# Attention, low-rank token mixing, a two-layer product and a gated projection on one core: weights of the first group prepared in attention, sums of u kept in DRAM, value weights and gates moved in the job list

## The chip, the cores and the metric

One core of one Trainium2 chip runs the whole program. The time is the device time of one execution in microseconds (us); the kernel before was timed in three runs, and one further execution was profiled. PE is TensorE, DVE is VectorE, ACT is ScalarE, SP is SyncE, whose queue issues nearly all the DMAs here, in program order.

## What is computed

```python
# 4 batches, 12 heads, 448 tokens, 64 per head; d_model 768
scores = scale * np.matmul(q, k.transpose(0, 1, 3, 2)) - np.log(S)
x  = np.matmul(1 / (1 + np.exp(-scores)), v)        # -> (4, 448, 768)
u  = x + (x.transpose(0, 2, 1) @ U @ V).transpose(0, 2, 1)   # rank 32
x  = u + np.maximum(u @ w_ch1, 0.0) @ w_ch2          # 768 -> 3072 -> 768
gate = sigmoid(causal 5-tap convolution of x along the tokens)
out  = (gate * (x @ w_val)) @ w_out                  # 768 -> 768 -> 768
```

All inputs and the output are float64 outside; on the chip a 64-bit word is turned into a 32-bit one, and each operand of a product is cut into a high and a low part.

## The kernel before

**Products.** `mm3` makes one product tile of three matmuls (high by high, high by low, low by high; lines 335, 336 and 337, 128x128 weights by 128x448). A weight's 128x384 half block is an operand tile of two parts. It comes to be in these steps: a DMA of 384 KB (`raw_w`), an activation on ACT (`unpack`, L90) and two operations on DVE (L91, L92) that make 32-bit words, a copy to the high part on ACT (L183), and a subtraction for the low part on DVE (L186). `keep` puts the 32-bit words into DRAM (192 KB) for the second pass.

**Stages.** Attention runs in 12 rounds of two heads' pairs each. `side` is a table of extra work: `side[q, k]` runs in round q at place k. Then come two passes, p=0 over batches 0 and 1 and p=1 over batches 2 and 3. A pass has six groups q of four column blocks of the hidden 3072. A group is two `chain`s, each of seven block products with the w1 operands A11, A12, S2, S1, S3, S4, A22 (S: sums of blocks of w1) and the u operands B11, B21, T2, T1, T3, B22, T4 (T: sums of blocks of u), which leave four h tiles per batch, and then four `ch2` (two halves of w2's columns by two batches) of four weights each. `ch2` adds its PSUM banks onto x (L732, "evict" below). After p=1 come the value product (`val`) and the output product (`fin`).

**Order of the work around.** There is no scheduler: the order of the code is the order on each engine. A list `jobs`, filled by `plan`, holds the preparation of all weights in the order of the list; `step()` is called after each block product of a chain and after each weight of a `ch2` (30 times in a group), and takes one job from the list by `pump`, if no more than ten weight tiles are then live. `weight(key)` is called in front of a product; if its operand has not been made, it takes jobs from the list there and then, up to the one that makes it:

```python
    def weight(*key):
        while key not in forms:
            if deferred:
                flush()
            else:
                pump(True)
        return forms[key]
```

`deferred` holds second halves of jobs (the low parts, mostly), which are written out at the next flush. A job of `pair_jobs` makes w1's operands for a chain (two at a time, with the S sums), `second_jobs` the w2 weights of a group. In p=1 they come out of DRAM as 32-bit words, unpacked before. In p=1, `plan` put into each group's list, between the pair jobs and in front of `second_jobs`, four jobs that prepare a half block of w_val or w_out and put it into DRAM (`last_jobs`, later fetched by `fetch`), and in q=1, 2 and 3 two gates' convolutions for batches 0 and 1 (`gate_jobs`: four operations on 128x896 on DVE, L790, two on ACT, and a put of 448 KB).

**The sums of u.** `u_sums` makes T1 to T4 of a row block k: four subtractions (L486) and four cuts in two (a copy on ACT, L472, and a subtraction on DVE, L473). B11, B21 and B22 are cut from u as they are (`u_plain`). For p=1 both were in a list `rush`, filled at the end of the last chains of p=0; `step()` takes two parts of it at a time, and takes no job from `jobs` in most of these steps.

Of the kernel before, what the change touches and what calls it, by code (L numbers as in the profile page):

```python
# [8 lines left out]
F32 = mybir.dt.float32  # L9
F32R = mybir.dt.float32r  # L10
U32 = mybir.dt.uint32
# [34 lines left out]
def tile_kernel(  # L46
# [38 lines left out]

    def unpack(raw, x, r):


        low, high = raw[:, :, 0], raw[:, :, 1]
        nc.scalar.activation(f32(x), f32(high), AF.Prelu, scale=2.0 ** -112, alpha=-(2.0 ** 32))  # L90
        nc.vector.tensor_scalar(r, low, 2.0 ** -29, 7.0, op0=ALU.mult, op1=ALU.min)  # L91
        nc.vector.scalar_tensor_tensor(  # L92
            x, x, 3, r, op0=ALU.logical_shift_left, op1=ALU.bitwise_or
        )
# [206 lines left out]
    def last_jobs(kind, n, half):  # L301
# [12 lines left out]
            deferred.append(lambda: in_two(x, t, done))  # L314
        return 1, job

    def weight(*key):
        while key not in forms:
            if deferred:
# [150 lines left out]
    def u_part(key, k, t, x):  # L470
        us[key, k] = t
        nc.scalar.activation(t[:, 0], x, AF.Copy)  # L472
        deferred.append(lambda: nc.vector.tensor_sub(t[:, 1], x, f32(t[:, 0])))  # L473
# [3 lines left out]
        b, d = halves[p][i], k + KH * j  # L477
        u_part((p, name), k, operand(f"{name}_{p}_{k}"), x_of(b, d))

    def u_sums(p, k):  # L480
# [12 lines left out]
        def cut(name):  # L493
            u_part((p, name), k, operand(f"{name}_{p}_{k}"), t[name])

        def first():
            both("T1", "T2")
            difference("T1", u[1, 0], u[0, 0])
            difference("T2", u[1, 1], t["T1"])

        def second():
            both("T4", "T3")
            difference("T4", u[0, 1], t["T2"])
            deferred.append(lambda: (cut("T2"), cut("T1")))

        def third():
            difference("T3", u[1, 1], u[1, 0])
            deferred.append(lambda: (cut("T3"), cut("T4")))

        return [first, second, third]  # L510

    def load_mix():
        nu, nk = NSC * RANK, KC * TAPS
# [335 lines left out]
    def attention_phase():  # L849


        ahead = range(3)
        for p in ahead[:2]:
            load_pair(p)
        nc.vector.memset(bias, -math.log(S))
        warm = scratch("warm")[:, :1]
# [9 lines left out]
        for p in ahead[2:]:  # L866
            load_pair(p)
        consts = load_mix()
        steps = prep_mix(*consts)
        side = {(0, 2): steps[:1], (1, 1): steps[1:2], (1, 2): steps[2:]}  # L870
# [9 lines left out]
            ):  # L880
                side[at] = some
        rounds = NP // 2
        at = iter([(9, 0), (9, 1), (9, 2), (10, 0), (10, 1), (10, 2), (11, 0)])
        todo = [part for k in range(KH) for part in u_sums(0, k)]
        side[9, 0] = todo[0:1]
        side[9, 1] = todo[1:2]
        side[9, 2] = todo[2:4]
        side[10, 0] = todo[4:5]
        side[10, 1] = todo[5:6] + [load_next] * RAWS
        side[10, 2] = todo[6:8]  # L890
        side[11, 0] = todo[8:9] + [pump]
        side[11, 1] = [pump] * 3
# [35 lines left out]
        values(NP - 1)  # L928
        attend_rest(rounds - 1)

    def plan():

        for p in range(2):
            for q in range(NQ):
                more = []
# [5 lines left out]
                new = []  # L941
                for c in (QUAD * q, QUAD * q + 2):
                    new += pair_jobs(p, c)
                    take = more[:len(more) // 2] if c % QUAD == 0 else more
                    more = more[len(take):]
                    for what, i in take:
                        if what == "st":
                            n, half = divmod(i, 2)
                            kind, n = ("val", n) if n < KC else ("out", n - KC)
                            new.append(last_jobs(kind, n, half))  # L950
                        else:
                            new += gate_jobs(halves[0], i)
                new += second_jobs(p, q)
                jobs.extend(new)

    def main_phase():

        sides = {}
        for q, b in enumerate(halves[1]):
            at = ((q, 4), (q, 5), (q + 1, 0), (q + 1, 1), (q + 1, 2))  # L960
            sides.update(zip(at, mix_units(b)))
        rush = []

        def step():
            if rush:
                for part in rush[:2]:
                    part()
                del rush[:2]
                if len(rush) % 4 == 0:
                    pump()  # L970
            else:
                pump()

        lists = {}

        def gate_half():
            i, k = divmod(open_at[0], 2)
# [18 lines left out]
        for p, bs in enumerate(halves):  # L996
            for q in range(NQ):
                last = q == NQ - 1
                events = iter(range(6))

                def side():
                    for unit in sides.pop((q, next(events)), ()):
                        unit()

                for i in range(2):
                    if last and i:
                        chain(p, QUAD * q + 2, step)
                    else:
                        chain(p, QUAD * q + 2 * i, step)
                    side()  # L1010
                if last and p == 0:
                    for name in ("B11", "B21"):
                        rush += [lambda name=name, k=k: u_plain(1, name, k) for k in range(KH)]
                    for k in range(KH):
                        rush += u_sums(1, k)
                    rush += [lambda k=k: u_plain(1, "B22", k) for k in range(KH)]
                if last and p:
                    for b in halves[0]:
                        for m in range(KC):
                            rush.append(lambda b=b, m=m: (  # L1020
                                y_split(b, m), deferred.append(lambda: y_low((b, m)))
                            ))
# [49 lines left out]
    with tc.manual_schedule():  # L1072
# [6 lines left out]
        for name, bufs in (("kept", 2 * NF), ("stash", 4 * KC), ("gates", KC)):  # L1079
# [60 lines left out]
```

## Time and profile before

| | us |
|---|---|
| median of three runs | 1055.39 |
| lowest and highest run | 1050.72, 1058.94 |
| profiled execution | 1057.33 |
| its span (first to last instruction) | 1055.5 |
| PE busy in the span | 1016.9 |
| DVE busy | 683.0 |
| ACT busy | 444.3 |

In the trace the attention ends, and the first product of p=0 begins, at 149.18 us; the last group of p=0 is at work from about 455 to 520 us; val and fin take the last stretch from about 866 us. A time such as "at 602" below is such a time from the start of the span.

### The profile page before, as it was taken

What the parts mean: (1) busy time and instruction counts of PE and PEld (TensorE: products, weight loads), DVE (VectorE), ACT (ScalarE), POOL (GpSimd) and SP (SyncE); (2) the same over time, 40 slices, a digit from 0 to 9 for tenths busy, and PEclk for the clock granted to TensorE, in tenths of its full rate; (3) what the DMA queues carried; (4) which work ended last, traced back from release to release, by engine and by line L of the source; (5) the groups of instructions that cost most, each with busy time, mean ns of one, the idle gap of its engine ahead of it and who ended that gap; (6) DMA issues with size and microseconds to landing.
All of it is one profiled execution on the core that took longest, in us unless ns stands there. A gap on an engine that the chain in (4) does not pass through costs nothing.

```text
span 1055.5 us, 14327 instructions
## 1 busy us (share of the span) xinstructions
PE 1016.9 (96%) x5289; PEld 860.4 (82%) x5289; DVE 683.0 (65%) x1293; ACT 444.3 (42%) x822; POOL 1.0 (0%) x6
## 2 busy tenths in 40 slices
PE   9999998999999999999799799897999999999998
PEld 5545457987879999999699698796999999999997
DVE  5455887868687787869976858667585748732100
ACT  6656774344352535445443525234251543301211
POOL 0000000000000000000000000000000000000000
PEclk9999999999999999999999899898999999999999
DMA  7444454738355464645243323234241426333441
GB/s 192 116 106 106 118 161 132 223 99 235 99 152 168 119 211 131 220 112 158 90 150 120 122 91 140 87 125 141 90 150 59 152 91 209 120 116 111 159 143 70
DMA packets 70086, 142.27 MB, mean 135 GB/s; under 512 B 13328, under 2 KB 34768, under 8 KB 70016
## 3 DMA queue, kind: packets, MB, share of 16 engines
q1 hardware_dynamic: 69744, 141.01, 44.0%
q8 instruction: 41, 0.67, 0.3%
q14 instruction: 29, 0.24, 0.1%
q10 hardware_dynamic: 224, 0.23, 0.1%
q0 software_dynamic: 48, 0.11, 0.0%
HBM read 104.76 MB, written 36.57 MB: 134 GB/s over the span
## 4 chain that ended last, share of the span: by engine, by line
PE 47%; DVE 5%; ACT 2%; issue 0%; DMA 0%; SPq 0%; ACTq 0%
PE ch L335 6%; PE ch L336 6%; PE ch L337 6%; PE fin L336 3%; PE fin L335 3%; PE val L336 3%; PE val L335 3%; PE fin L337 3%; PE val L337 3%; DVE g L790 3%; PE x L335 2%; PE x L337 2%; PE x L336 2%; PE z L336 1%; PE z L337 1%; PE z L335 1%
## 5 line engine op out<-in xcount | busy, mean ns | idle before, releaser
L335 PE MATMUL ch<-h,w 128*128 128x448 f32 x576 | 217.4, 377 | 26.7 <-ACT w L183 17.5
L337 PE MATMUL ch<-h,w 128*128 128x448 f32 x576 | 215.3, 374 | 0.5 <-DVE w L186 0.4
L336 PE MATMUL ch<-h,w 128*128 128x448 f32 x576 | 215.6, 374 | 0.0
L335 PEld LDWEIGHTS ch<-h,w 128*128 128x128 f32 x576 | 111.4, 193 | 40.1 <-ACT w L183 18.6
L732 DVE TENSOR_TENSOR xs<-ch,xs 128x448 f32<-128x448 f32 x144 | 86.0, 621 | 61.7 <-PE ch L337 61.3
L337 PEld LDWEIGHTS ch<-h,w 128*128 128x128 f32 x576 | 111.2, 193 | 11.7 <-DVE w L186 1.4
L336 PEld LDWEIGHTS ch<-h,w 128*128 128x128 f32 x576 | 111.5, 194 | 10.0
L92 DVE SCALAR_TENSOR_TENSOR x_w<-x_w,r_w 128x384 uint32<-128x384 uint32 x96 | 53.7, 559 | 34.8 <-ACT x_w L90 29.6
L400 ACT ACTIVATE a<-sc,bias 128x896 f32<-128x896 f32 x72 | 67.2, 1008 | 8.5 <-PE sc L412 8.4
L443 PE MATMUL av<-a,vr 128*64 128x448 f32 x288 | 59.7, 548 | 1.0 <-ACT a L400 1.0
L335 PE MATMUL x<-T,S 128*128 128x448 f32 x144 | 53.7, 373 | 4.2 <-ACT S L183 3.3
L834 ACT ACTIVATE o<-fin 128x448 f32<-128x448 f32 x23 | 12.6, 546 | 106.8 <-PE fin L337 104.0
L90 ACT ACTIVATE x_w<-raw_w 128x384 f32<-128x384 f32 x96 | 51.6, 543 | 10.3 <-DMA raw_w<-in_w 7.9
L412 PEld LDWEIGHTS sc<-ks 64*128 64x128 f32 x432 | 37.6, 184 | 21.8 <-issue 5.4
L412 PE MATMUL sc<-ks 64*128 64x448 f32 x432 | 52.3, 380 | 1.4 <-DVE xs L624 0.7
L337 PE MATMUL x<-T,S 128*128 128x448 f32 x144 | 53.2, 369 | 0.0
L336 PE MATMUL x<-T,S 128*128 128x448 f32 x144 | 53.2, 369 | 0.0
L335 PE MATMUL val<-y,f_val 128*128 128x448 f32 x144 | 53.0, 368 | 0.0
L336 PE MATMUL val<-y,f_val 128*128 128x448 f32 x144 | 53.0, 368 | 0.0
L337 PE MATMUL val<-y,f_val 128*128 128x448 f32 x144 | 53.0, 368 | 0.0
L335 PE MATMUL fin<-z,f_out 128*128 128x448 f32 x144 | 53.0, 368 | 0.0
L336 PE MATMUL fin<-z,f_out 128*128 128x448 f32 x144 | 53.0, 368 | 0.0
(199 smaller groups left out, 1937.3 us busy)
## 6 DMA issues: line engine op xcount, KB each, us to landing
raw_w<-in_w SPq DMA_DIRECT2D x96, 384.0 KB, 4.1
kq<-in_kq SPq DMA_DIRECT2D x47, 224.0 KB, 3.7
k_w<-x_w SPq DMA_DIRECT2D x48, 192.0 KB, 3.9
k_h<-x_w SPq DMA_DIRECT2D x48, 192.0 KB, 4.5
raw_x_w<-k_w SPq DMA_DIRECT2D x24, 384.0 KB, 3.8
f_val<-s_val SPq DMA_DIRECT2D x24, 384.0 KB, 3.0
f_out<-s_out SPq DMA_DIRECT2D x24, 384.0 KB, 3.5
out_t<-o SPq DMA_DIRECT2D x11, 448.0 KB, 2.8
```

The lines of the kernel that those rows point to most:

```text
L90: nc.scalar.activation(f32(x), f32(high), AF.Prelu, scale=2.0 ** -112, alpha=-(2.0 ** 32))
L92: nc.vector.scalar_tensor_tensor(x, x, 3, r, op0=ALU.logical_shift_left, op1=ALU.bitwise_or)
L335: mm(ps, wk[:, 0], x[:, 0], start=start, stop=False, **kw)
L336: mm(ps, wk[:, 0], x[:, 1], start=False, stop=False, **kw)
L337: mm(ps, wk[:, 1], x[:, 0], start=False, stop=stop, **kw)
L400: nc.scalar.activation(a[:, :, :], ps[:, :, :S], AF.Sigmoid, bias=bias, scale=1.0 / math.sqrt(D))
L412: mm(ps[:, h, :S].rearrange("p (c s) -> p c s", c=NSC), ks[r, tk, 0, c], ks[r, tq, 1, :, :SC], start=t == 0, stop=t == 2,)
L443: mm(att["ps"][D * h:D * h + D, :S], vr[:, h, c], a[:, h], start=c == 0, stop=False,)
L732: nc.vector.tensor_add(y, ps[j], y)
L790: nc.vector.scalar_tensor_tensor(t[0], y(k), tap(k), t[0], op0=ALU.mult, op1=ALU.add)
L834: nc.scalar.activation(o, ps, AF.Copy)
```

## The change

Four things are done. **First group's w2**: the eight w2 weights of p=0, q=0 and the first four half blocks of w_val are prepared at 13 places of rounds 2 to 8 of the attention (`ahead_jobs`, `side`) and put into DRAM as finished operand tiles; in q=0, `ready_jobs` fetches the eight w2 tiles where `second_jobs` stood. **Sums of u**: for p=1 they are made in groups 2, 3 and 4 of p=0 (`u_sums(1, k, True)`), put into DRAM (`parked`) and fetched by `u_fetch` from the last chain of p=0 on, from where `rush` now begins. **The list**: in p=1, `second_jobs` stands ahead of the gates and of the `last_jobs`; there is one gate in each group, and w_val and w_out share 20 jobs. **step**: fetches of `rush` no longer keep a step from taking a job, and steps 1, 4 and 7 of the run take two.

```diff
+    def ahead_jobs(kind, n, half):
+        key = kind, n, half
+        loads.append(key)
+        def first():
+            raw = loaded.pop(key)
+            x, r = (...)
+            words_of(raw, x, r)
+        def second():
+            join(x, r)
+            load_next()
+            t = operand("%s_%d_%d" % key)[:, :, :HQ]
+            def low():
+                nc.vector.tensor_sub(t[:, 1], x, f32(t[:, 0]))
+                if kind == "w2":
+                    keep((f"h{half}_", n // 2), n % 2, x)
+                deferred.append(put)
+            def put():
...
+                nc.sync.dma_start(stash[key][:, :, :], f32(t))
+            nc.vector.tensor_copy(t[:, 0], x)
+            low()
+    def ready_jobs():
+        def job(n, half):
+            def run():
+                t = wtile(f"w2_0_{n}_{half}")
+                nc.sync.dma_start(f32(t), stash["w2", n, half][:, :, :])
+                forms[0, n, half] = t
...
+            if park:
+                deferred.append(lambda: put(name, w))
+        def put(name, w):
+            parked[name, k] = s = pools["parked"].tile(...)
+            nc.sync.dma_start(s[:, :, :], f32(w[:, :, :]))
...
+        slots = [(q, k) for q in range(2, 9) for k in (0, 2)]
+        for at, key in zip(slots, early_keys):
+            first, second = ahead[key]
+            side[at] = then + [first] + side.get(at, [])
+            then = [second]
...
         for p in range(2):
             for q in range(NQ):
-                if p:
-                    n = KC * 2 * 2 // NQ
-                    more += [("st", i) for i in range(q * n, (q + 1) * n)]
-                    if 1 <= q < 1 + KH:
-                        more += [("gate", 2 * (q - 1)), ("gate", 2 * (q - 1) + 1)]
...
+                for c in (QUAD * q, QUAD * q + 2):
+                    jobs.extend(pair_jobs(p, c))
+                jobs.extend(ready_jobs() if p == q == 0 else second_jobs(p, q))
+                if p:
+                    if q < KC:
+                        jobs.extend(gate_jobs(halves[0], q))
+                    for _ in range(4):
+                        if more:
+                            jobs.append(last_jobs(*more.pop(0)))
...
+        for k in range(KH):
+            parts = u_sums(1, k, True)
+            sides[2 + k, 4] = parts[:2]
+            sides[2 + k, 5] = parts[2:]
...
         def step():
-            if rush:
-                for part in rush[:2]:
-                    part()
-                del rush[:2]
-                if len(rush) % 4 == 0:
-                    pump()
-            else:
+            now = rush[:2]
+            del rush[:2]
+            for busy, part in now:
+                part()
+            done[0] += 1
+            if not any(busy for busy, _ in now):
                 pump()
+                if done[0] in (1, 4, 7):
+                    pump()
...
-                if last and p == 0:
-                    for name in ("B11", "B21"):
-                        rush += [lambda name=name, k=k: u_plain(1, name, k) for k in range(KH)]
-                    for k in range(KH):
-                        rush += u_sums(1, k)
-                    rush += [lambda k=k: u_plain(1, "B22", k) for k in range(KH)]
```

The new `rush`, in front of the second chain of the last group: B11 and B21 (busy), T2 and T1 and T3 (fetches), B22 (busy), T4 (fetches).

**Place 1: ACT, second chain of the first group of p=0.** Before (p1, u2 and p5 are copies of a chain's PSUM sums, h its results; the numbers behind a name are pass and column block, the last one a buffer):

```order
L183 ACTIVATE A12_0_2_1823<-x_w1_2_1_1802 128x384
L681 ACTIVATE h1_1_1825<-p5_0_0_1800 128x448
L90 ACTIVATE x_w1_3_0_1838<-raw_w1_3_0_1695 128x384
L681 ACTIVATE h1_0_1858<-x_0_0_1736 128x448
L90 ACTIVATE x_w1_3_1_1860<-raw_w1_3_1_1785 128x384
L681 ACTIVATE h0_1_1869<-u2_0_0_1778 128x448
L676 ACTIVATE p1_0_2_1882<-x_0_2_1867 128x448
L681 ACTIVATE h2_0_1901<-p1_0_2_1882 128x448
L183 ACTIVATE S2_0_2_1904<-x_w1_2_0_1780 128x384
L183 ACTIVATE S1_0_2_1906<-s1_0_2_1884 128x384
```

Now, at the same products:

```order
L190 ACTIVATE A11_0_2_1968<-x_w1_2_0_1926 128x384
L190 ACTIVATE A12_0_2_1970<-x_w1_2_1_1947 128x384
L95 ACTIVATE x_w1_3_0_1972<-raw_w1_3_0_1853 128x384
L95 ACTIVATE x_w1_3_1_1994<-raw_w1_3_1_1931 128x384
L748 ACTIVATE h1_1_2001<-p5_0_0_1966 128x448
L748 ACTIVATE h1_0_2027<-x_0_0_1894 128x448
L190 ACTIVATE S2_0_2_2031<-x_w1_2_0_1926 128x384
L190 ACTIVATE S1_0_2_2033<-s1_0_2_2013 128x384
L748 ACTIVATE h0_1_2037<-u2_0_0_1945 128x448
L743 ACTIVATE p1_0_2_2051<-x_0_2_2035 128x448
L190 ACTIVATE S3_0_2_2053<-x_w1_3_0_1972 128x384
```

S2_0_2 stood behind the copy p1_0_2 and the result h2_0 of its own chain's first products; now it stands ahead of that copy.

**Place 2: DVE, second group of p=1** (g0_0 and g0_1 are the gates of row blocks 0 and 1; w2_1_4_0 is the group's first w2 weight, h4 to h7 its h tiles, xs the x tiles). Before:

```order
L687 TENSOR_TENSOR p1_1_6_5945<-p1_1_6_5945,y_1_6_5955 128x448
L790 SCALAR_TENSOR_TENSOR g0_0_5967<-xs_61,cw_62,g0_0_5967 128x896 x4
L682 SCALAR_TENSOR_TENSOR h6_2_5987<-p1_1_6_5945,h6_2_5987 128x448
L687 TENSOR_TENSOR p5_1_6_5998<-p5_1_6_5998,x_1_6_5928 128x448
L790 SCALAR_TENSOR_TENSOR g0_1_6013<-xs_61,cw_62,g0_1_6013 128x896 x3
L682 SCALAR_TENSOR_TENSOR h7_3_6017<-p5_1_6_5998,h7_3_6017 128x448
L687 TENSOR_TENSOR u2_1_6_5983<-u2_1_6_5983,z_1_6_5929 128x448
L790 SCALAR_TENSOR_TENSOR g0_1_6013<-xs_61,cw_62,g0_1_6013 128x896
L682 SCALAR_TENSOR_TENSOR h7_2_6042<-x_1_6_5928,h7_2_6042 128x448
L682 SCALAR_TENSOR_TENSOR h6_3_6048<-u2_1_6_5983,h6_3_6048 128x448
L186 TENSOR_TENSOR w2_1_4_0_6055<-raw_x_h0__2_1_5913,w2_1_4_0_6055 128x384
L186 TENSOR_TENSOR w2_1_5_0_6056<-raw_x_h0__2_1_5913,w2_1_5_0_6056 128x384
```

Now:

```order
L749 SCALAR_TENSOR_TENSOR h6_2_6089<-p1_1_6_6056,h6_2_6089 128x448
L193 TENSOR_TENSOR w2_1_4_1_6102<-raw_x_h1__2_1_6010,w2_1_4_1_6102 128x384
L193 TENSOR_TENSOR w2_1_5_1_6103<-raw_x_h1__2_1_6010,w2_1_5_1_6103 128x384
L754 TENSOR_TENSOR p5_1_6_6100<-p5_1_6_6100,x_1_6_6038 128x448
L749 SCALAR_TENSOR_TENSOR h7_3_6121<-p5_1_6_6100,h7_3_6121 128x448
L754 TENSOR_TENSOR u2_1_6_6087<-u2_1_6_6087,z_1_6_6039 128x448
L193 TENSOR_TENSOR w2_1_6_1_6132<-raw_x_h1__3_1_6045,w2_1_6_1_6132 128x384
L193 TENSOR_TENSOR w2_1_7_1_6133<-raw_x_h1__3_1_6045,w2_1_7_1_6133 128x384
L749 SCALAR_TENSOR_TENSOR h7_2_6151<-x_1_6_6038,h7_2_6151 128x448
L857 SCALAR_TENSOR_TENSOR g0_1_6153<-xs_61,cw_62,g0_1_6153 128x896 x3
L749 SCALAR_TENSOR_TENSOR h6_3_6158<-u2_1_6_6087,h6_3_6158 128x448
L857 SCALAR_TENSOR_TENSOR g0_1_6153<-xs_61,cw_62,g0_1_6153 128x896
```

The two gates stood ahead of all eight w2 weights; now one stands there, behind the eighth (w2_1_7_1), and w2_1_4_0 (six rows ahead of the first one shown) has come in front of all of the second chain's results.

**Place 3: DVE, last group of p=0, around the evicts of `ch2`.** Before, at the second evict:

```order
L235 TENSOR_TENSOR s1_1_0_5154<-raw_x_w1_1_1_5017 128x384
L236 TENSOR_TENSOR raw_x_w1_1_1_5017<-raw_x_w1_0_1_4986,raw_x_w1_1_1_5017 128x384
L473 TENSOR_TENSOR T2_1_1_5132<-T1_T2_1_1_5103,T2_1_1_5132 128x448
L473 TENSOR_TENSOR T1_1_1_5134<-T1_T2_1_1_5103,T1_1_1_5134 128x448
L473 TENSOR_TENSOR T3_1_1_5136<-T4_T3_1_1_5127,T3_1_1_5136 128x448
L473 TENSOR_TENSOR T4_1_1_5138<-T4_T3_1_1_5127,T4_1_1_5138 128x448
L486 TENSOR_TENSOR T4_T3_1_2_5152<-xs_61 128x448
L473 TENSOR_TENSOR T2_1_2_5161<-T1_T2_1_2_5149,T2_1_2_5161 128x448
L473 TENSOR_TENSOR T1_1_2_5163<-T1_T2_1_2_5149,T1_1_2_5163 128x448
L732 TENSOR_TENSOR xs_61<-ch2_0_5_1_0_0_5081,xs_61 128x448
L732 TENSOR_TENSOR xs_61<-ch2_0_5_1_0_1_5082,xs_61 128x448
L732 TENSOR_TENSOR xs_61<-ch2_0_5_1_0_2_5083,xs_61 128x448
```

Now, at the first evict:

```order
L193 TENSOR_TENSOR w2_0_22_0_5140<-x_w2_22_0_5141,w2_0_22_0_5140 128x384
L527 TENSOR_TENSOR B22_1_0_5168<-xs_61,B22_1_0_5168 128x448
L527 TENSOR_TENSOR B22_1_1_5184<-xs_61,B22_1_1_5184 128x448
L527 TENSOR_TENSOR B22_1_2_5186<-xs_61,B22_1_2_5186 128x448
L96 TENSOR_SCALAR r_w2_23_0_5205<-raw_w2_23_0_5093 128x384
L99 SCALAR_TENSOR_TENSOR x_w2_23_0_5204<-x_w2_23_0_5204,r_w2_23_0_5205 128x384
L193 TENSOR_TENSOR w2_0_23_0_5203<-x_w2_23_0_5204,w2_0_23_0_5203 128x384
L96 TENSOR_SCALAR r_w2_20_1_5227<-raw_w2_20_1_5117 128x384
L99 SCALAR_TENSOR_TENSOR x_w2_20_1_5226<-x_w2_20_1_5226,r_w2_20_1_5227 128x384
L799 TENSOR_TENSOR xs_61<-ch2_0_5_0_0_0_5148,xs_61 128x448
L799 TENSOR_TENSOR xs_61<-ch2_0_5_0_0_1_5149,xs_61 128x448
L799 TENSOR_TENSOR xs_61<-ch2_0_5_0_0_2_5150,xs_61 128x448
```

The subtractions and low parts of T1 to T4 that stood between the evicts are gone from here; two of the group's w2 weights (w2_23_0 and the words of w2_20_1), which were ready ahead of the first evict and of all of u's parts, stand now directly in front of that evict, behind B22.

## Rows read from the trace of the kernel before

**Rows 1.** The page's first part: busy us (share of the span) xinstructions.

```profile
PE 1016.9 (96%) x5289; PEld 860.4 (82%) x5289; DVE 683.0 (65%) x1293; ACT 444.3 (42%) x822; POOL 1.0 (0%) x6
```

**Rows 2.** Waits of PE: engine, line, waited for: us in total, times, longest.

```profile
PE ch L335 <- ACT w L183: 17.5, 3, 5.8
PE ch L335 <- DVE xs L732: 7.5, 2, 4.9
PE x L335 <- ACT S L183: 3.3, 1, 3.3
PE ch L335 <- DVE h L682: 1.7, 1, 1.7
...
PE x L335 <- ACT p L676: 0.8, 1, 0.8
```

**Rows 3.** Windows: length, busy PE PEld DVE ACT POOL, PEclk, DMA share, GB/s.

```profile
168.60:172.00 3.40, 2.80 (x8) 2.40 (x9) 1.56 (x3) 0.96 (x3) 0.00 (x0) 0.50 0.00 0
253.90:257.30 3.40, 2.99 (x8) 2.68 (x9) 3.31 (x8) 0.80 (x2) 0.00 (x0) 0.51 0.90 338
312.00:315.40 3.40, 3.40 (x10) 3.01 (x11) 3.27 (x8) 0.09 (x1) 0.00 (x0) 0.50 0.62 216
506.50:509.90 3.40, 3.03 (x8) 2.76 (x9) 3.37 (x7) 1.77 (x5) 0.00 (x0) 0.50 0.00 0
598.70:605.50 6.80, 3.31 (x9) 2.92 (x10) 6.00 (x11) 4.00 (x8) 0.00 (x0) 0.50 0.35 125
663.50:670.30 6.80, 5.52 (x15) 4.87 (x16) 4.83 (x10) 4.23 (x9) 0.00 (x0) 0.50 0.63 215
728.40:735.20 6.80, 5.99 (x16) 5.32 (x17) 4.35 (x9) 3.76 (x9) 0.00 (x0) 0.50 0.69 234
519.00:522.40 3.40, 3.17 (x16) 2.95 (x17) 3.40 (x8) 2.01 (x5) 0.00 (x0) 1.00 0.93 333
```

**Rows 4.** Timeline around 600 us: start, us, engine, line, operation [idle before <-releaser].

```profile
595.09 3.52 DVE L790 SCALAR_TENSOR_TENSOR g<-xs,cw,g 128x896 f32<-128x896 f32 x3 [0.89 <-ACT g L794]
...
601.63 0.92 ACT L183 ACTIVATE w<-raw_x_h__2_1_5913 128x384 fp32r<-128x384 f32 x2
...
602.19 0.74 PE L335 MATMUL ch<-h,w 128*128 128x448 f32 x1 [5.85 <-ACT w L183]
```

**Rows 5.** Timeline at the first product of p=0, and at 168 us.

```profile
149.18 0.47 PE L335 MATMUL x<-B,A 128*128 128x448 f32 x1
...
168.16 0.58 ACT L681 ACTIVATE h<-p 128x448 fp32r<-128x448 f32 x1 [3.49 <-DVE p L687]
```

**Rows 6.** Groups on DVE by form: shapes xcount | busy us, mean ns | idle before.

```profile
L92 DVE SCALAR_TENSOR_TENSOR x_w<-x_w,r_w 128x384 uint32<-128x384 uint32 x96 | 53.7, 559 | 34.8 <-ACT x_w L90 29.6
L91 DVE TENSOR_SCALAR r_w<-raw_w 128x384 uint32<-128x384 uint32 x96 | 34.0, 354 | 0.8 <-DMA raw_w<-in_w 0.2
...
L790 DVE SCALAR_TENSOR_TENSOR g<-xs,cw,g 128x896 f32<-128x896 f32 x24 | 27.6, 1150 | 3.2 <-ACT g L794 2.7
L186 DVE TENSOR_TENSOR w<-x_w,w 128x384 fp32r<-128x384 f32 x48 | 26.5, 551 | 0.0
...
L486 DVE TENSOR_TENSOR T_T<-xs,T_T 128x448 f32<-128x448 f32 x12 | 7.5, 623 | 0.3
```

**Rows 7.** Groups on ACT by form: mean of L90 and L183.

```profile
L90 ACT ACTIVATE x_w<-raw_w 128x384 f32<-128x384 f32 x96 | 51.6, 543 | 10.3 <-DMA raw_w<-in_w 7.9 <-issue 2.2
...
L183 ACT ACTIVATE w<-x_w 128x384 fp32r<-128x384 f32 x48 | 25.2, 526 | 36.5 <-DVE x_w L92 36.5
```

**Rows 8.** Windows of attention's rounds 2 to 5, of the first group, and of groups 3 to 5.

```profile
22.00:74.00 52.00, 52.00 (x389) 26.59 (x387) 28.98 (x60) 33.20 (x41) 0.00 (x0) 1.00 0.51 124
...
180.00:200.00 20.00, 19.54 (x95) 17.27 (x94) 18.38 (x40) 9.99 (x21) 0.00 (x0) 1.00 0.93 284
...
335.00:447.00 112.00, 112.00 (x552) 103.03 (x551) 85.93 (x178) 49.81 (x104) 0.00 (x0) 1.00 0.57 170
```

**Rows 9.** DMA issues: out<-in queue operation xcount, KB each, median us to landing.

```profile
raw_w<-in_w SPq DMA_DIRECT2D x96, 384.0 KB, 4.1
```

More of the change, by code (lines that the diff above doesn't have):

```diff
@@ L315, in last_jobs @@
         return 1, job
+    def ahead_jobs(kind, n, half):
+        key = kind, n, half
+        loads.append(key)
+        got = []
+        def first():
+            raw = loaded.pop(key)
+            x, r = (
+                pools[k].tile([P, HQ], U32, tag=k, name="%sa_%s_%d_%d" % (k, *key))[:, :] for k in "xr"
+            )
+            words_of(raw, x, r)
+            got.extend((x, r))
+        def second():
+            x, r = got
+            join(x, r)
+            load_next()
+            x = f32(x)
+            t = operand("%s_%d_%d" % key)[:, :, :HQ]
[5 more added lines that the diff above has]
+            def put():
+                stash[key] = pools["stash"].tile([P, 2, HQ], F32, tag="stash", name="s_%s_%d_%d" % key)
+                nc.sync.dma_start(stash[key][:, :, :], f32(t))
+            nc.vector.tensor_copy(t[:, 0], x)
+            low()
+        return first, second
+    def ready_jobs():
[4 more added lines that the diff above has]
+                forms[0, n, half] = t
+            return 1, run
+        return [job(n, half) for half in range(2) for n in range(QUAD)]
     def weight(*key):
@@ L510, in u_sums, with u_fetch @@
         return [first, second, third]
+    parked = {}
+    def u_fetch(name, k):
+        us[(1, name), k] = t = operand(f"{name}_1_{k}")
+        nc.sync.dma_start(f32(t[:, :, :]), parked[name, k][:, :, :])
     def load_mix():
@@ L849, in attention_phase @@
     def attention_phase():
-        ahead = range(3)
-        for p in ahead[:2]:
+        for p in range(2):
             load_pair(p)
@@ L865, in attention_phase @@
         prep_pair(0)
-        for p in ahead[2:]:
-            load_pair(p)
+        load_pair(2)
         consts = load_mix()
@@ L888, in attention_phase @@
         side[10, 0] = todo[4:5]
[L889 removed]
+        side[10, 1] = todo[5:6]
         side[10, 2] = todo[6:8]
@@ L929, in attention_phase @@
         attend_rest(rounds - 1)
+    early_keys = [("w2", n, half) for half in range(2) for n in range(QUAD)]
+    early_keys += [("val", n, half) for n in range(2) for half in range(2)]
+    ahead = {}
     def plan():
+        for key in early_keys:
+            ahead[key] = ahead_jobs(*key)
+        more = [("val", n, half) for n in range(2, KC) for half in range(2)]
+        more += [("out", n, half) for n in range(KC) for half in range(2)]
         for p in range(2):
             for q in range(NQ):
-                more = []
+                for c in (QUAD * q, QUAD * q + 2):
+                    jobs.extend(pair_jobs(p, c))
+                jobs.extend(ready_jobs() if p == q == 0 else second_jobs(p, q))
                 if p:
-                    n = KC * 2 * 2 // NQ
-                    more += [("st", i) for i in range(q * n, (q + 1) * n)]
-                    if 1 <= q < 1 + KH:
-                        more += [("gate", 2 * (q - 1)), ("gate", 2 * (q - 1) + 1)]
[L941 to L950, printed above, removed]
-                        else:
-                            new += gate_jobs(halves[0], i)
-                new += second_jobs(p, q)
-                jobs.extend(new)
+                    if q < KC:
[3 more added lines that the diff above has]
+                            jobs.append(last_jobs(*more.pop(0)))
     def main_phase():
@@ L1005, in main_phase @@
                 for i in range(2):
[L1006 to L1009, printed above, removed]
-                    side()
-                if last and p == 0:
-                    for name in ("B11", "B21"):
-                        rush += [lambda name=name, k=k: u_plain(1, name, k) for k in range(KH)]
-                    for k in range(KH):
-                        rush += u_sums(1, k)
-                    rush += [lambda k=k: u_plain(1, "B22", k) for k in range(KH)]
+                    if last and i and p == 0:
+                        plain = lambda *names: [
+                            (1, lambda n=n, k=k: u_plain(1, n, k)) for n in names for k in range(KH)
+                        ]
+                        again = lambda *names: [
+                            (0, lambda n=n, k=k: u_fetch(n, k)) for n in names for k in range(KH)
+                        ]
+                        rush += plain("B11", "B21") + again("T2", "T1", "T3") + plain("B22") + again("T4")
+                    chain(p, QUAD * q + 2 * i, step)
+                    side()
                 if last and p:
```

21 lines of the change are left out of this document (13 added, 8 removed).

## The prediction, made before the changed kernel ran

> **What bounds the kernel now.** I read the page's busy shares first, then the waits of PE, then windows of the stretches in which the granted clock falls, then the timeline at the longest wait. PE is busy 1016.9 of 1055.5 us [rows 1], so what a change of order can win lies in the 38.6 us in which it is not, and in what the clock takes after them. The waits list shows where these are [rows 2]: 17.5 us in three waits of `ch2`'s first product for a w2 weight's high part from ACT, 7.5 in two for an evict, 3.3 for S2, 1.7 for an h, 0.8 for a p. The clock is the second half of the loss. The windows [rows 3] show it at 0.50 (1.2 instead of 2.4 GHz) for 6.8 us at each of the three long waits and for 3.4 us from about the end of each of the waits of 3.3, 2.6 (7.5 less 4.9), 1.7 and 4.9 us; after the wait of 0.8 us (519) it stays at 1.00. Work at half clock takes twice the time, so half of PE's busy time in such a window is lost: 3.31/2 + 5.52/2 + 5.99/2 = 7.4 us at the three, 2.80/2 = 1.4 at 169, 3.03/2 = 1.5 at 507.
>
> The timeline at 602 [rows 4] says why PE waited: DVE is in a gate's taps (3.52 us for three of them, a fourth later), the w2 copy on ACT starts at 601.63 and PE at 602.19. PE needs that weight while the list still has gates in front of it (place 2): `weight` then makes everything up to it at once, and h and gates share DVE with it.
>
> **The change part by part.** Durations are of the profiled execution, 1057.33 us; it is 1.94 above the runs' median, which comes off at the end.
>
> *The list in p=1.* In the second group the first w2 weight stood behind eight gate operations on DVE; now it stands ahead of the second chain's results, and the gate comes after all eight weights. By the order, every w2 weight of p=1 is now written out at least six steps of some 1.8 us before its product. The 17.5 us and the 7.4 of clock go: −24.9 us. Where the gates go: a group's first two `ch2`, 8 steps or 14.6 us, now hold on DVE one gate (4 × 1.15), the words and low parts of two half blocks (2 × (0.35 + 0.56 + 0.55)), two evicts (6 × 0.62, the form of L486's row) and six low parts or sums for the next chain (6 × 0.55), 14.5 us in all (pieces: [rows 6]). DVE has no room left there, so evicts slip; but eight PSUM banks rotate, and an evict may come one whole `ch2` late (7.3 us) before the third `ch2` wants its bank. I put 1 us for it: the range is 0 to 4, a tail as the 1.7 and 0.8 waits [rows 2] in some groups. The gates' puts and the val loads join SP behind the pass's w2 loads and ahead of the next group's w1 loads, which are due six steps later.
>
> *The first group.* At 169 PE waits for S2's high part on ACT. ACT stood in h2_0 (3.49 us idle for a p from DVE [rows 5]) in front of it: S2 was made only when PE asked for it, so it stood behind the results of products that PE had just done (place 1). Now two jobs are taken at steps 1, 4 and 7, no w2 weight is unpacked there, and S2 stands ahead of p1_0_2; it is written out two products earlier. The wait goes with its clock: 3.3 + 1.4 = 4.7 us.
>
> *What that costs in attention.* Twelve half blocks: on ACT 0.54 each [rows 7], on DVE 0.35 + 0.56 + a copy + 0.55 [rows 6]. No row shows a 128x384 copy on DVE; it lies between 0.35 and 0.56 of other operations on that shape, and I take 0.35, the row of one input without a second operand. That is 1.8 us of DVE and 0.54 of ACT per place of half a round, some 6.2 us (149 us [rows 5] by 12 rounds, halved). PE is busy all 52 of 52 us in these rounds, DVE 28.98, ACT 33.20 [rows 8]: with the new work DVE goes to about 0.85, ACT to 0.72. If that cover were not there, 12 × 1.8 = 22 us would be at stake. The DMAs are closer: for w2 a load of 384 KB, a keep of 192 and a put of 384, 0.98 MB per 6.2 us or 160 GB/s, on top of 124: 284 GB/s. The fetches in the first group moved 284 GB/s at a share of 0.93 [rows 8], and 338 at 0.90 [rows 3], so the demand stands at what the trace has shown, not beyond. On SP, a put waits for DVE's low part, and the next round's q and k loads stand behind it; it is written out a flush after that part, which mostly spares the wait. I put 1.5 us, between 0 and 3 (a load's 4.1 us [rows 9], once late and partly covered). The Trainium skill gives about 358 GB/s as what one core has of its memory ("HBM Reference", "Specifications (TRN2)"); by that figure the attention would have room for all of it, and the term would be an estimated 0 instead of 1.5; the highest window here, 338, does not contradict it.
>
> *The sums of u in groups 2 to 4.* They add to DVE 4 subtractions and 4 low parts a group, 8 × 0.62 = 5.0 us of a group's 55, and four puts of 448 KB. DVE is busy 85.93 of 112 us there and PE 112.00 [rows 8]: nothing of it shows in the sum. Without that cover it would be 15 us over three groups.
>
> *From p=0 to p=1.* Before, PE lost 4.9 us to the second evict, which stood on DVE behind the sums of u (place 3), 1.5 of clock, and 0.8 later: 7.2. The 24 operations are gone from there. What is late next are w2 weights: the busy steps for B11, B21 and B22 take no job, so A22 and w2_20 to w2_22 of half 0 are written out two steps ahead instead of five, and w2_23 only when PE asks. From the end of the chain ACT has two h, three B22 copies, two copies of w2 and a word (some 5 us of 0.53 to 0.58 each), with DVE's parts in between about 6.5, while PE gets there after 3 × 1.8 = 5.5. I put 0.5 + 0.5 + 1.7 for three short waits and 1.4 for one stretch of half clock: 4 us, between 1 and 15. The gain is 3.2 of the 7.2.
>
> *Left as they are:* the waits at 254 (2.6) and 312 (1.7), of an evict and an h in groups 1 and 2: the mixing of batches 2 and 3 puts its DVE work there, before as after. If the shift by one step undoes them, up to 2.6 + 1.7 + 1.5 + 1.7 = 7.5 us come on top (half of 2.99 and of 3.40 us of busy PE at half clock [rows 3]).
>
> The sum: −24.9 + 1.0 − 4.7 + 1.5 − 3.2 = −30.3, or 1027.0 beside the profiled 1057.33, and 1025 beside the median.
>
> A drop of the clock followed each wait of 1.7 us or more, and none followed 0.8 [rows 2, 3]; that is why the transition has one such stretch in it and not three. The Trainium skill tells of matmul groups between which short idles come so often that the clock swings, though no single idle is long ("TensorE: Matmul & The Clock Gate", "A second HAM failure mode: psum-queue depth-cycling"); by that the three short waits in a row would cost an estimated two stretches more, 3 us. No row here shows short waits in such a row.
>
> **The rivals.** *The transition becomes the bound* (14 in 100). Twelve fetches of 448 KB, the last raw w2 loads and the first words of p=1 share one SP queue: 12 × 448 + 5 × 384 + 8 × 192 KB are 9 MB in 30 us, 300 GB/s, and each fetch also waits until PE has left its tile, so a raw w2 load behind it waits too. For it: 0.93 was already the share at 519, where loads bunch [rows 3]. Against: fetched tiles are wanted only 15 us later. One wait like those of 5.8 us costs with its clock 5.8 + 3.0; one to two in place of the 4 us give 1030 to 1039, 1034 in the middle.
>
> *Attention is bound by its DMAs* (10 in 100). If the share grows with bytes, 124 GB/s at 0.51 means that 243 are all there is [rows 8]. Then 52 us become 52 × 284/243, 8.8 more instead of 1.5: 1032. Against it stands the 284 of the first group.
>
> *The waits of p=1 come back elsewhere* (9 in 100). The list is moved, but the step from DVE's 14.5 of 14.6 to a wait is short. It decides from 6.7 us of backlog on (7.3 less an evict's 0.62); then three or four of the groups lose 5.8 us and clock again, and the time is 1045 to 1053, within one per cent.
>
> *Slower* (3 in 100): the attention waits for q and k in each of rounds 2 to 7. To end above 1066 it must lose 42 us, 7 per round of 12.4, so the DMA would have to deliver below 3.5 MB in 19.4 us or 180 GB/s with the puts among the loads. The rows show 284; only writes, which are few in attention now, could do it.
>
> **How the numbers follow.** The forecast's own case has 64 in 100, at 1025. One per cent, about what a measurement of this kernel can tell from no change, lies at 1045 and 1066. Faster: 64 + 14 + 10 = 88; same 9; slower 3. For the range: below, the transition without loss (−4), no cost in attention or ch2 (−2.5) and the two waits at 254 and 312 partly gone (−4.5) give 1014; above, the first two rivals with their upper ends, and both together, give 1041. About 1 in 10 lies above (the last two rivals), and less below.
>
> **What would show it.** In the trace after: no wait of `ch` for a w2 part in groups 1 to 3 of p=1, clock 1.00 there, and the gates' taps inside `ch2`. No wait for S in the first group. PE busy throughout attention, with a DMA share near 0.9 in rounds 2 to 5; first product still at 149 to 152 us. At the end of p=0, waits for w2_23 of about 2 us and not for an evict. The waits in groups 1 and 2 of p=0 stand. I would be wrong by most if a raw w2 load stood behind a blocked fetch, or if PE waited for evicts behind the gates in every group of p=1.

## The result, and the profile after

The changed kernel takes 1028.08 us (median of four runs, 1025.57 to 1029.73) against 1054.45 of the kernel before (four runs): a ratio of 0.9746, 95% interval 0.9702 to 0.979. 1025 was forecast, from 1014 to 1041. The sum came out; the term for the attention and some smaller ones did not. The line numbers of the changed kernel are 7 to 67 higher (L183 is now L190, L335 L389, L732 L799). One execution of the experiment e5 below (1047.4 us) fell in the chip's slow state and is left out of its median and range.

The page's busy times after, beside [rows 1], and the waits of PE, beside [rows 2]:

```profile
PE 1003.6 (98%) x5289; PEld 855.2 (83%) x5289; DVE 685.2 (67%) x1305; ACT 437.0 (43%) x810; POOL 1.0 (0%) x6
```

```profile
PE sl L482 <- DVE xs L691: 5.5, 3, 3.1
PE sc L466 <- ACT al L454: 3.4, 1, 3.4
PE ch L389 <- DVE xs L799: 2.0, 1, 2.0
PE ch L389 <- DVE h L749: 1.7, 1, 1.7
PE sc L466 <- DVE xt L650: 1.5, 1, 1.5
...
PE x L389 <- DVE p L754: 1.2, 1, 1.2
PE ch L389 <- ACT w L190: 1.1, 1, 1.1
...
PE x L389 <- ACT p L743: 0.7, 1, 0.7
```

The 17.5 us for a w2 weight in p=1 are gone, the 4.9 for an evict and the 3.3 for S2 too. New are waits of sl and sc: these are the attention's products, which had next to none before. The first product of p=0 shows what they cost, 164.33 against 149.18 us [rows 5], 15.15 us later, and the windows of the rounds with the added work say so too (busy PE, DVE and ACT, clock, DMA share, GB/s, beside [rows 8]):

```profile
164.33 0.47 PE L389 MATMUL x<-B,A 128*128 128x448 f32 x1
```

```profile
22.00:74.00 52.00, 47.08 (x338) 24.27 (x339) 30.72 (x68) 32.03 (x42) 0.00 (x0) 0.97 0.78 204
74.00:98.00 24.00, 20.20 (x140) 9.86 (x138) 20.28 (x44) 14.23 (x20) 0.00 (x0) 0.93 0.90 254
```

338 matmuls in place of 389 in the same 52 us, and twice the clock falls for 3.4 us (36.8 and 91.4).

Where the 27.5 us between the two spans (1055.5 and 1028.0) come from, from the waits and half of PE's busy time at half clock:

| stretch | before | after | difference |
|---|---|---|---|
| start to the first product of p=0 | 149.2 | 164.3 | +15.2 |
| first group: S2 and its clock; p after | 3.3 + 1.4 | 1.2 + 0.7 | −2.8 |
| groups 1 and 2: evict and h, clock | 2.6 + 1.5 + 1.7 + 1.7 | 2.0 + 1.7 + 1.7 | −2.1 |
| end of p=0 | 4.9 + 1.5 + 0.8 | 1.1 | −6.1 |
| p=1 | 17.5 + 7.4 | 0 | −24.9 |
| sum | | | −20.7 |

Some 7 us are in no wait. Most of them are in PE's pace. The value and output products, for which PE never waits, take 182.2 us to the end of the run in the trace of before (from 873.34) and 178.7 in that of after (from 849.31). With the clock at 1.00 and PE busy throughout, a window of 100 us late in the run holds 486 matmuls before and 496 after. Each trace has stretches of both paces (50 us of before with 248), at other places each time:

```profile
540.00:590.00 50.00, 50.00 (x248) 46.35 (x247) 32.72 (x62) 18.34 (x37) 0.00 (x0) 1.00 0.35 116
880.00:980.00 100.00, 100.00 (x486) 90.81 (x485) 51.20 (x70) 18.18 (x29) 0.00 (x0) 1.00 0.38 125
```

```profile
400.00:450.00 50.00, 50.00 (x244) 45.37 (x243) 41.76 (x87) 25.34 (x52) 0.00 (x0) 1.00 0.70 214
860.00:960.00 100.00, 100.00 (x496) 92.65 (x495) 47.78 (x67) 18.31 (x31) 0.00 (x0) 1.00 0.38 123
```

That is 2 per cent, up to 17 us over the 860 us of p=0 to fin if a run had one pace and another the other. In the experiments below times of two kernels are therefore compared together with their traces, stretch by stretch.

What the attention waits for can be read at one of its waits. PE stands 3.1 us at 90.79 behind an addition of the mixing on DVE; DVE had stood 3.41 us in a cast of the next q and k, behind a DMA, and does the added block's work before the addition, all in order:

```profile
86.60 0.63 DVE L434 CAST ks<-kq 128x896 fp32r<-128x896 f32 x1 [3.41 <-DMA kq<-in_kq]
...
88.39 0.55 DVE L99 SCALAR_TENSOR_TENSOR xa_w<-xa_w,ra_w 128x384 uint32<-128x384 uint32 x1
88.97 0.36 DVE L355 CAST w<-xa_w 128x384 fp32r<-128x384 f32 x1
...
90.11 1.68 DVE L691 TENSOR_TENSOR xs<-h,xs 128x448 f32<-128x448 f32 x3
```

```profile
90.79 1.23 PE L482 MATMUL sl<-kq 64*64 64x448 f32 x8 [3.10 <-DVE xs L691]
```

And why the q and k come late, on SP's queue in the round from 42 to 56 us (a row is an issue, with its length on SP):

```profile
42.31 0.61 SPq L417 DMA_DIRECT2D vr<-in_va  x1
47.06 0.55 SPq L421 DMA_DIRECT2D vl<-in_va  x1
47.73 0.52 SPq L153 DMA_DIRECT2D raw_w<-in_w  x1
48.34 0.38 SPq L186 DMA_DIRECT2D k_h<-xa_w  x1
48.82 0.60 SPq L353 DMA_DIRECT2D s_w<-w  x1
49.55 0.55 SPq L153 DMA_DIRECT2D raw_w<-in_w  x1
50.21 0.61 SPq L186 DMA_DIRECT2D k_h<-xa_w  x1
51.34 0.56 SPq L353 DMA_DIRECT2D s_w<-w  x1
52.00 0.60 SPq L414 DMA_DIRECT2D kq<-in_kq  x1
```

SP stands from 42.9 to 47.06 in front of a load of vl (32 KB). There are two vl tiles, and the load waits for PE's last matmuls (L510, `attend_rest`) of the round whose tile it takes. In the trace of before it waits as well, up to 7 us at a time, and then the next kq goes out 1.1 us after it (54.36 and 55.46). Now the six DMAs of two blocks have piled up behind the vl load and go first; kq follows 4.9 us after it.

### The profile page after: what moved, and what is told of

It is laid out like the page before. It is cut to its first block, busy times and chain, and to the rows that moved or that the text cites. A ratio compares the mean times of both kernels' runs of the same rounds, so it can differ in the third digit from the quotient of the medians.

```text
span 1028.0 us, 14405 instructions
## 1 busy us (share of the span) xinstructions
PE 1003.6 (98%) x5289; PEld 855.2 (83%) x5289; DVE 685.2 (67%) x1305; ACT 437.0 (43%) x810; POOL 1.0 (0%) x6
## 4 chain that ended last, share of the span: by engine, by line
PE 66%; DVE 1%; ACT 0%; issue 0%; DVEq 0%
PE ch L389 9%; PE ch L391 9%; PE ch L390 9%; PE x L390 4%; PE x L391 4%; PE x L389 4%; PE val L389 3%; PE fin L389 3%; PE fin L391 3%; PE fin L390 3%; PE val L390 3%; PE val L391 3%; PE z L391 2%; PE z L390 2%; PE z L389 2%; PE y L389 1%
## 5 line engine op out<-in xcount | busy, mean ns | idle before, releaser
L389 PE MATMUL ch<-h,w 128*128 128x448 f32 x576 | 212.4, 369 | 4.8 <-DVE xs L799 2.0
L391 PE MATMUL ch<-h,w 128*128 128x448 f32 x576 | 211.6, 367 | 0.1
L390 PE MATMUL ch<-h,w 128*128 128x448 f32 x576 | 211.4, 367 | 0.0
L389 PEld LDWEIGHTS ch<-h,w 128*128 128x128 f32 x576 | 108.6, 188 | 16.5 <-DVE xs L799 2.8
L391 PEld LDWEIGHTS ch<-h,w 128*128 128x128 f32 x576 | 108.6, 189 | 10.2 <-DVE w L193 1.0
L390 PEld LDWEIGHTS ch<-h,w 128*128 128x128 f32 x576 | 108.6, 189 | 9.0
L799 DVE TENSOR_TENSOR xs<-ch,xs 128x448 f32<-128x448 f32 x144 | 82.9, 618 | 34.5 <-PE ch L391 34.5
L99 DVE SCALAR_TENSOR_TENSOR x_w<-x_w,r_w 128x384 uint32<-128x384 uint32 x88 | 49.2, 559 | 25.9 <-ACT x_w L95 20.2
L466 PEld LDWEIGHTS sc<-ks 64*128 64x128 f32 x432 | 40.5, 197 | 26.9 <-issue 6.1
L466 PE MATMUL sc<-ks 64*128 64x448 f32 x432 | 55.1, 397 | 6.3 <-ACT al L454 3.4
L389 PE MATMUL x<-T,S 128*128 128x448 f32 x144 | 52.8, 367 | 0.7 <-ACT p L743 0.7
L389 PE MATMUL fin<-z,f_out 128*128 128x448 f32 x144 | 52.6, 365 | 0.0
L390 PE MATMUL fin<-z,f_out 128*128 128x448 f32 x144 | 52.6, 365 | 0.0
L391 PE MATMUL fin<-z,f_out 128*128 128x448 f32 x144 | 52.6, 365 | 0.0
L389 PE MATMUL val<-y,f_val 128*128 128x448 f32 x144 | 52.6, 365 | 0.0
```

The lines of the kernel that those rows point to most:

```text
L99: nc.vector.scalar_tensor_tensor(x, x, 3, r, op0=ALU.logical_shift_left, op1=ALU.bitwise_or)
L389: mm(ps, wk[:, 0], x[:, 0], start=start, stop=False, **kw)
L390: mm(ps, wk[:, 0], x[:, 1], start=False, stop=False, **kw)
L391: mm(ps, wk[:, 1], x[:, 0], start=False, stop=stop, **kw)
L466: mm(ps[:, h, :S].rearrange("p (c s) -> p c s", c=NSC), ks[r, tk, 0, c], ks[r, tq, 1, :, :SC], start=t == 0, stop=t == 2,)
L799: nc.vector.tensor_add(y, ps[j], y)
```

## The experiments

Theories on the attention: **queue** (the order on SP, as just read), **bytes** (the DMA engines are full), **DVE** (the added 1.8 us per place hold up evicts). On the rest: which of the change's parts carries which term.

**e1_list: the kernel before with the list of p=1 alone.** `plan` as in the changed kernel, but `second_jobs` in every group and all 24 half blocks in p=1.

```diff
-                    more += [("st", i) for i in range(q * n, (q + 1) * n)]
-                    if 1 <= q < 1 + KH:
-                        more += [("gate", 2 * (q - 1)), ("gate", 2 * (q - 1) + 1)]
...
+                jobs.extend(second_jobs(p, q))
+                if p:
+                    if q < KC:
+                        jobs.extend(gate_jobs(halves[0], q))
+                    for _ in range(4):
+                        if more:
+                            jobs.append(last_jobs(*more.pop(0)))
```

> The kernel before with one part of the change alone: in p=1 the pass's own w2 weights stand ahead of the gates and of the value and output weights, one gate a group. If the three waits of 17.5 us and their clock are the order of the list and nothing else, they go and nothing comes in their place: 24.9 us less than before, 1029 to 1031 beside 1054.5, with the waits at 169, 254, 312 and 507 us as before. If DVE cannot carry a gate inside the second product, the evicts of p=1 are waited for and less than 15 us come back: above 1040.

Measured: 1024.28 against 1051.66 us, ratio 0.9756 (0.9706 to 0.9807). That is 27.4 less, and below the expected 1029 to 1031. Its waits:

```profile
PE ch L335 <- DVE xs L732: 7.1, 2, 4.4
PE x L335 <- ACT S L183: 3.7, 1, 3.7
PE ch L335 <- DVE h L682: 1.7, 1, 1.7
```

The three waits for w2 are gone and nothing stands in their place; the others are as before. The waits and the clock account for 24.9 us of the gain; the profiled run was also almost wholly of the faster pace, which makes its span (1022.3) look better than this part deserves. This part alone is worth as much as the whole change: the other three parts together bring nothing, because the attention takes back what two of them gain (e5, e6 and e7 show which two).

**e2_no_early: the changed kernel without blocks prepared in the attention.**

```diff
-    early_keys = [("w2", n, half) for half in range(2) for n in range(QUAD)]
-    early_keys += [("val", n, half) for n in range(2) for half in range(2)]
+    early_keys = []
...
-                jobs.extend(ready_jobs() if p == q == 0 else second_jobs(p, q))
+                jobs.extend(second_jobs(p, q))
```

> The changed kernel with nothing prepared in the attention: the first group's w2 weights are unpacked in the first group, the first four half blocks of the value weights in p=1. If the attention's longer time (first product at 164.3 instead of 149.2 us) is the price of the twelve blocks, the first product stands at 149 to 150 us and the kernel takes 1013 to 1017 us; the first group may lose up to 4 us of this again. If the attention is longer for another reason, it stays at 164 and the time at 1028 to 1032.

Measured: first product at 149.62, as expected; 1024.58 us (1016.32 to 1025.69), ratio 0.9711 (0.9661 to 0.9761), 7.6 above the upper end of what was expected. Its profiled run was one of the slower pace: 485 matmuls in 860 to 960 us where the changed kernel's has 496. The attention's 15 us are gone, and the first group costs next to nothing more: no wait above 1.2 us there.

```profile
PE x L389 <- DVE p L754: 2.7, 3, 1.2
PE ch L389 <- DVE xs L799: 2.3, 1, 2.3
PE ch L389 <- DVE h L749: 1.7, 1, 1.7
...
PE ch L389 <- ACT w L190: 1.1, 1, 1.1
```

**e3_vl3: a third vl tile.**

```diff
-        for name, bufs in (("ks", 2), ("vr", 4), ("vl", 2)):
+        for name, bufs in (("ks", 2), ("vr", 4), ("vl", 3)):
```

> The changed kernel with three vl tiles instead of two, all else equal. Queue theory: the load of vl waits on SP for PE's last matmuls of an earlier round, the twelve blocks' loads and puts pile up behind it, and the next q and k loads behind these; with a third tile it does not wait, and the attention gets back at least half of its 15 us: first product at 150 to 157 us, kernel 1014 to 1021. Theory of bytes (the DMA engines are full) and theory of DVE (its extra work is in the way of evicts): first product within 2 us of 164, kernel 1026 to 1030.

Measured: 1015.74 us (1015.52 to 1015.86), ratio 0.9653 (0.9629 to 0.9677); first product at 150.09. The added blocks' bytes now move beside the rest at 259 GB/s with a share of 0.93, DVE does their work there too (38.82 us busy for 28.98 before), and PE loses nothing in 22 to 74:

```profile
22.00:74.00 52.00, 52.00 (x389) 26.53 (x389) 38.82 (x85) 36.40 (x49) 0.00 (x0) 1.00 0.93 259
```

So bytes and DVE both fall as causes. SP now has both pairs of q and k out ahead of the blocks, vl included, and no vl stands for PE:

```profile
47.00 0.54 SPq L414 DMA_DIRECT2D kq<-in_kq  x1
...
49.59 0.60 SPq L421 DMA_DIRECT2D vl<-in_va  x1
50.53 0.34 SPq L153 DMA_DIRECT2D raw_w<-in_w  x1
```

e2 and e3 also show what the pace is worth. Their spans are 1023.9 and 1014.0 us, their first products stand at 149.62 and 150.09, and their waits differ little. Late in the run e2 takes 520 us for 2518 matmuls and e3 takes 510 for as many, both without a wait at a clock of 1.00, e2's row first:

```profile
490.00:1010.00 520.00, 520.00 (x2518) 472.33 (x2517) 313.33 (x543) 183.03 (x360) 0.00 (x0) 1.00 0.40 131
490.00:1000.00 510.00, 510.00 (x2518) 472.60 (x2517) 308.79 (x532) 180.12 (x353) 0.00 (x0) 1.00 0.39 128
```

So the 9.9 us between the two spans are the pace, and not a cost of leaving the weights unprepared.

**e4_pool: the twelve blocks' DMAs on POOL's queue**, the keeps among them, with two vl tiles as before.

```diff
-            nc.sync.dma_start(r[:, :], w_io[kind][n][:, half * HQ:(half + 1) * HQ])
+            queue = nc.gpsimd if key in ahead else nc.sync
+            queue.dma_start(r[:, :], w_io[kind][n][:, half * HQ:(half + 1) * HQ])
...
-                nc.sync.dma_start(stash[key][:, :, :], f32(t))
+                nc.gpsimd.dma_start(stash[key][:, :, :], f32(t))
```

> The changed kernel with the loads, keeps and puts of the twelve blocks on POOL's own queue, the same bytes at the same places of the program. Queue theory: nothing of the twelve blocks stands ahead of the q and k loads, the attention ends 8 to 14 us earlier, first product at 150 to 156 us. Theory of bytes: the q and k loads land as late as now, first product at 162 to 167. Theory of DVE: the same 162 to 167, with q and k landing in under 4 us.

Measured: 1021.47 us, ratio 0.9727 (0.9677 to 0.9777); first product at 154.40. Where the remaining 5 us are lost:

```profile
0.00:12.00 12.00, 9.25 (x32) 5.98 (x33) 2.29 (x7) 5.08 (x6) 2.63 (x9) 1.00 0.82 223
...
24.00:98.00 74.00, 73.62 (x558) 38.04 (x550) 57.92 (x124) 51.71 (x68) 16.18 (x27) 1.00 0.87 237
```

In the first 12 us PE has done 32 matmuls, where the kernel before has 55: on a queue of their own the first three raw loads go out at 2.05 us and meet the first q and k loads. That these are what holds PE up is my reading; no run shows it apart. From 24 to 98, where the changed kernel loses most (PE busy 65.27 of 74 us), PE is busy 73.62 of 74 with the added blocks' DMAs in the same places of the program. Queue again, from another side.

**e5_no_park: the sums of u at the end of p=0, as before**, all else as changed. `rush` is filled behind the last chain with `u_sums(1, k)`, so it also begins a chain later than in the changed kernel, and every second of its steps takes a job again, as before.

> The changed kernel with the sums of u made at the end of p=0 as before (rush behind the last chain, nothing kept in DRAM), all else as changed. If parking is what removed the wait for an evict at the end of p=0, that wait is back: 4.5 to 5 us in ch and 0.8 in x, with 3.4 us of half clock, and the 1.1 us wait for w2_23 gone; 5 to 7 us more than the changed kernel: 1033 to 1035. If the transition is no longer bound by DVE for another reason (the list, the steps), no wait above 1.5 us is there and the time is within 2 us of 1028.

Measured: 1033.48 us (nine runs, 1030.44 to 1044.78), ratio 0.9848 (0.9805 to 0.989). The evict's wait is back with a long stretch of half clock:

```profile
PE ch L389 <- DVE xs L799: 6.3, 2, 4.4
```

```profile
517.20:524.00 6.80, 5.68 (x15) 5.07 (x16) 6.77 (x14) 4.24 (x10) 0.00 (x0) 0.50 0.00 0
```

4.4 + 5.68/2 = 7.2 us against 1.1 in the changed kernel: parking, with the earlier `rush` that goes with it, is what the end of p=0 gains by.

**e6_no_double and e7_ready_no_double: one job a step everywhere**, once with nothing prepared ahead (e2's kernel), once with all twelve blocks (e3's).

```diff
                 pump()
-                if done[0] in (1, 4, 7):
-                    pump()
```

> The kernel without any block prepared in the attention (the second experiment), and with one job a step everywhere (no second job at steps 1, 4 and 7). If the wait for S2 in the first group was removed by the doubled steps and not by the prepared weights, it is back: 3.3 to 3.7 us in x behind S, and 3.4 us of half clock, some 4 us more than the second experiment's trace at the same place. If it was the freed engines of the first group, nothing changes there, since these are not freed in either.

> The changed kernel with three vl tiles (the third experiment), with all twelve blocks prepared in the attention, and one job a step everywhere. If the prepared weights are enough to remove the wait for S2, there is none above 1.5 us in the first group, and the time is that of the third experiment, 1014 to 1017. If the doubled steps did it, the wait of 3.3 to 3.7 us and its half clock are back: 4 to 5 us more, 1018 to 1021.

Measured: 1025.94 us, ratio 0.9762 (0.9696 to 0.9828), and 1019.66, ratio 0.9735 (0.9667 to 0.9803). Both traces have the same line, here that of e7:

```profile
PE x L389 <- ACT S L190: 3.7, 1, 3.7
```

S2 is waited for whether w2 is prepared or not, and is not waited for with the doubled steps whether w2 is prepared (e3) or not (e2). The doubled steps remove the wait; the prepared weights have no part in it. From the first product to the end of the second group's wait for an evict it is 105.9 us in e6 (150.26 to 256.13) and 105.5 in e7 (150.16 to 255.69), against 100.7 in e2 and 100.6 in e3: the doubled steps are worth some 5 us. The medians of e6 and e2 do not show it (1025.94 and 1024.58); e6's profiled run was of the faster pace late in the run (495 matmuls in 860 to 960), e2's of the slower.

**e8_mix and e9_vl3_mix: the mixing of batches 2 and 3 one place earlier**, on e2's and on e3's kernel.

```diff
-            at = ((q, 4), (q, 5), (q + 1, 0), (q + 1, 1), (q + 1, 2))
+            at = ((q, 3), (q, 4), (q, 5), (q + 1, 0), (q + 1, 1))
```

> The second experiment (nothing prepared ahead) with the mixing of batches 2 and 3 in p=0 one place earlier, so that its last additions come behind the second group's first chain and not between two second products. If the wait at 250 us (2.3, with half clock) comes of these additions taking PSUM banks and DVE between two second products, it goes: 3 to 4 us less than the second experiment at that place; the wait for an h at 307 of 1.7 stays or goes with it. If not, both stand, and the earlier transposes may add waits of up to 3 us in the first group.

> The third experiment (three vl tiles, all else as changed) with the mixing of batches 2 and 3 one place earlier, as in the eighth. If the earlier place only moves the evict's wait of 2 to 2.6 us by one second product, as the eighth showed, the time is that of the third experiment within 2 us, 1013 to 1018. If the prepared weights leave DVE enough room in the first group for the earlier place, the wait with its half clock goes: 1010 to 1013.

Measured: 1019.33 us, ratio 0.9704 (0.9637 to 0.9771), and 1013.7 (six runs, 1011.8 to 1016.57), ratio 0.9624 (0.9588 to 0.966). The waits of e9:

```profile
PE ch L389 <- DVE xs L799: 4.2, 1, 4.2
PE x L389 <- DVE p L754: 2.7, 3, 1.4
```

The h is no longer waited for, but the evict is waited for longer (4.2 for 2.0; in e8 2.6 for 2.3). The wait moved and did not go. That e9 is the fastest of all is within what the pace can do, its profiled span (1014.5) is no shorter than e3's (1014.0), and no gain of the earlier place is shown.

## Why the prediction was right, and where it was not

*The list in p=1* was sized right: −24.9 forecast, and 17.5 + 7.4 gone in the trace, with e1 as the proof that this part does it alone. The 1.0 for evicts slipping behind the gates was not needed: no evict of p=1 is waited for, the slack of one `ch2` was enough.

*Attention* is the step that failed: "it is written out a flush after that part, which mostly spares the wait. I put 1.5 us, between 0 and 3". It cost 15.2 us, beyond even the rival's 8.8, and two of the prediction's own signs failed with it: PE busy throughout attention, and a first product at 149 to 152 us. I looked at DVE, ACT and bytes, and on SP only at the new puts' own waits. What I passed over is a wait that was there already and cost nothing: SP stood up to 7 us at a time in front of vl, and nothing but early loads stood behind it. The six DMAs of a round went into that gap, and q and k behind them left 4.9 us later; DVE, ACT and PE then stood in order behind them. The rival (attention bound by its DMAs) named the right stage with the wrong reason: its rule (share grows with bytes, 243 GB/s at most) is refuted by the 259 GB/s of e3. What bound here was an order, not a rate. The Trainium skill gives about 358 GB/s as what one core has of its memory ("HBM Reference", "Specifications (TRN2)"); e3, which lost nothing at 259, and the highest window read here, 352 (91.4 to 94.8 us of the changed kernel), do not contradict it, and by it the term would have been an estimated 0.

*The first group*: 4.7 us were forecast; the table has 2.8, since two short waits for a p came in place of the one for S2. The reason was half wrong. "two jobs are taken at steps 1, 4 and 7, no w2 weight is unpacked there": only the first half works (e2, e6, e7). The weights prepared in attention, the first item of the change, bring nothing measurable: from the first product to the end of the second group's wait for an evict it is 100.7 us in e2 (149.62 to 250.30) and 100.6 in e3 (150.09 to 250.72).

*From p=0 to p=1*: the mechanism was right (e5), the size was not. I left 4 us there; 1.1 is left, the wait for w2_23 alone, without a drop of the clock. A22 and w2_20 to w2_22, two steps ahead, came in time.

*The waits in groups 1 and 2* stand, as forecast: 2.0 and 1.7, one of them without its drop of the clock. *The sums of u in groups 2 to 4* cost nothing, as forecast: PE waits nowhere from 323 to 495 us.

So by the terms the gain was 9.6 us smaller than forecast (20.7 for 30.3): attention +13.7, the first group +1.9, the end of p=0 −2.9, evicts −1.0, groups 1 and 2 −2.1. What is in no wait, mostly PE's pace, gave some 7 of these back in the profiled runs. The total was right partly by luck.

Three sums of the prediction are a little off, without effect on its outcome. Work at half clock does not take twice the time: at 312 us before, a matmul starts every 0.37 us (312.64, 313.01, 313.38), which is 1.8 times the 203 to 207 ns at full clock, so the clock's terms, and those of the table, are about a tenth too large. The eight ACT operations at the end of p=0 come to 4.4 us and not to 5. And the upper end of 1041 takes the first rival at its middle, 1034, with the second's 7.3; with both upper ends it would be 1046.

## What to carry to other kernels

Before work with DMAs is put into a stretch that looks free, read that stretch's in-order DMA queue: a wait there that costs nothing today becomes the place where everything new piles up, ahead of the loads that the next stage needs. Such a wait may be one small buffer away from gone (here 32 KB loads into a third tile: 12 us). And when a change has several parts, give each a run of its own: here one part alone was worth as much as the whole, and the part named first gained nothing and cost what two others had won.

## What the runs showed of the hardware

At a granted clock of 1.00 and without a wait, PE's matmuls of 448 columns come at one of two paces, about 203 ns (510 us with 2518, e3) and 207 ns (520 us with 2518, e2), in stretches of under ten to over 500 us that lie elsewhere in each run. In the two windows of e2 and e3 above, DVE, ACT and the DMAs do nearly the same; the cause stays open.

A wait near 1.7 us is followed by half clock in some traces and not in others. Eight traces have one of 1.64 to 1.68 us for an h at the same products; a drop follows in three (before [rows 3], e1, e5) and none in five (after, e2, e4, e6, e7). In e7 there is none even after 2.6 us. Below are the 3.4 us after the wait of 1.7 in the changed kernel, and those after the 2.6 in e7:

```profile
322.30:325.70 3.40, 3.38 (x17) 3.14 (x18) 3.31 (x7) 0.43 (x1) 0.00 (x0) 1.00 0.67 238
```

```profile
255.70:259.10 3.40, 3.40 (x16) 3.10 (x17) 3.31 (x7) 0.00 (x0) 0.00 (x0) 1.00 0.78 276
```

What decides it stays open. The prediction's reading that a drop followed each wait of 1.7 us or more held for the one trace it came from; the drop after such a wait is not a price to put down in full.
